# Two-kilobyte rows for the first weight slices, a new order of the start-up and heavier transfer costs in a planned kernel

## The chip, the cores and the metric

The kernel runs on one core of a Trainium2 chip. The core has a matrix engine (TensorE, PE in the profile), a vector engine (DVE), a scalar engine (ACT), GpSimd (POOL) and SyncE (SP), which issues nearly all transfers; 16 DMA engines carry them. The time is device microseconds of one execution; the kernel before took a median of 743.23 us in 3 runs (741.82 to 743.35).

## The reference

Attention between tokens and a small state comes first, in both directions; two dense layers follow. For batch 4, 8 heads, 512 tokens, 32 state rows and head size 64:

```
scores  = scale * x @ state^T          a  = softmax(scores)    xread = a  @ state
scores2 = scale * state @ x^T          a2 = softmax(scores2)   sread = a2 @ x
t   = concat(xread, sread) as [2176, 512]         (4 x 544 rows)
y   = g1(t @ w_in1) @ w_out1          g1(h) = h if h > 0 else exp(h) - 1
out = g2(y @ w_in2) @ w_out2          g2(h) = h * tanh(softplus(h))
```

All four weights are [512, 2048] or [2048, 512] and come as 64-bit floats; activations are 32-bit.

## The kernel before

The tokens' part of the first layer is not computed as written. A head's `a @ state` followed by its rows of `w_in` is `a @ (state @ w_in)`, so the kernel folds the state into the weight (`fold`, L532, result tile `m`) and multiplies the softmax weights (`x1`) by it. The hidden dimension is cut into 16 slices of 128 columns; slice j of `w_in` gives hidden tile h_j (`mm1`), an activation chain on ACT and DVE (`hidden`) turns it into g_j, and `mm2` adds g_j @ w_out slice j into four accumulators.

A slice of `w_in1` is loaded by `weight`: two DMAs, one for partitions 0 to 63 and one for 64 to 127, each of 64 partitions x 4 rows of 128 values (1 KB a row, from a matrix whose rows are 16 KB). Then ACT (`Prelu`, L467), a DVE shift and a DVE merge (L484) make 32-bit floats of the 64-bit words. A `w_out` slice is one DMA over 128 partitions with rows of 4 KB. Raw words go to `raw_in` and `raw_out` tiles; tokens come to `xb` tiles (`load_x`, L565: 128 partitions, rows of 1 KB).

A softmax of one half of the heads of one batch (`token_reads`): transpose tokens on PE (`xT`), scores on PE, then on DVE the maximum, the difference, the sum and the division, `exp` on ACT, a transpose on PE (`pT`) and a copy to `x1`. The raw scores are copied too (`raw`), stored to DRAM (`s2d`) and read again later in the other direction. State rows come through `st_raw` and `st` to the tiles `sd`.

The order of all instructions is written by a planner (`Plan.run`): it simulates the engines with a cost for each operation, picks whichever ready operation can start first (ties by due time), and emits it. A transfer costs its KB times a weight, at 330 KB/us in one line of transfers, plus 2 us; small idle stretches of PE up to plan time 18 are filled with dummy transposes (`gap`). What the planner believes of a transfer therefore sets the order of PE, ACT, DVE and SP, and each engine runs that order strictly. On the chip, eight semaphores take turns with the DMAs, so SP issues a DMA only when the eighth before it has landed.

Of the kernel before, what the change touches and what calls it, by code (L numbers as in the profile page):

```python
# [11 lines left out]
F32 = mybir.dt.float32  # L12
F32R = mybir.dt.float32r
U32 = mybir.dt.uint32
I64 = mybir.dt.int64
AF = mybir.ActivationFunctionType
ALU = mybir.AluOpType
# [5 lines left out]
P = 128  # L23
B, H, S, NS, D = 4, 8, 512, 32, 64
DM, DFF = 512, 2048
ST = S + NS
NK = DM // P
NF = DFF // P
# [29 lines left out]
class Plan:  # L58
# [10 lines left out]
    def add(self, engs, cost, fn, r=(), w=(), due=None, lag=0.0, after=(), place=()):  # L69


        op = Op()
        op.engs = (engs,) if isinstance(engs, str) else engs
        op.cost, op.fn, op.due, op.lag = cost, fn, due, lag
        op.succs, op.end, op.seq = [], None, len(self.ops)
        preds = set(after)
        for k in r:
            if k in self.writer:
                preds.add(self.writer[k])
        for k in w:  # L80
            if k in self.writer:
                preds.add(self.writer[k])
            preds.update(self.readers.get(k, ()))
        for k in w:
            self.writer[k], self.readers[k] = op, []
        for k in r:
            if k not in w:
                self.readers.setdefault(k, []).append(op)
        preds.discard(op)
        op.preds = preds  # L90
        for p in preds:
            p.succs.append(op)
        op.n = len(preds)
        bufs = {}
        for k in (*r, *w):
            k = k[0] if isinstance(k, tuple) else k
            if isinstance(k, Buf):
                bufs[k] = None
        bufs.update((k, None) for k in place)
        op.bufs = list(bufs)  # L100
        for b in op.bufs:
            b.left += 1
        self.ops.append(op)
        return op
# [112 lines left out]
def attention_elu_mish(  # L217
# [18 lines left out]
    nc = tc.nc  # L236
    w_dram = {1: (w_in1, w_out1), 2: (w_in2, w_out2)}
# [3 lines left out]
    def add(*args, after=(), **kw):  # L241
        return plan.add(*args, after=(*after, *gate), **kw)
# [23 lines left out]
    def buf(pool, tag, bufs, shape, dt=F32, name=None):  # L266
        return Buf(pool, tag, bufs, shape, dt, f"{name or tag}{next(serial)}")

    EITHER = ("ACT", "DVE")
# [4 lines left out]
    def copy(e, o, i):  # L274
        (nc.scalar.copy if e == "ACT" else nc.vector.tensor_copy)(o, i)
# [7 lines left out]
    def both(n):  # L283
        return {"ACT": act(n), "DVE": dve(n)}
# [5 lines left out]
    SP, ACTQ = "SP", "ACTQ"  # L290
# [37 lines left out]
    for s, (kind, blk, t0, n, j) in enumerate(steps):  # L328
        c = mm1_cost(kind, blk, n, j) + (mm2_cost(kind, n, whole_out(kind, blk, j)) if kind < 2 else n * 3 * mm(DM))
# [21 lines left out]
    early = True  # L351
# [30 lines left out]
    def A(*args, **kw):  # L382
        op = add(*args, **kw)
        attention.append(op)
        return op
# [46 lines left out]
        return w1[j // 2].t.rearrange("p (k f) -> p k f", k=NK)[:, k, j % 2 * P:(j % 2 + 1) * P]  # L432

    loads = itertools.count()

    def weight(kind, layer, j, due=None):
        i = next(loads)
        soon = i < EARLY
        due = -20.0 + i if i < RAW_FIRST else due
        name = f"{kind}{layer}_{j}_"  # L440
        raw = buf("w", "w_out", NF, [P, DM], I64, "raw_" + name) if soon else \
            buf("work", "wraw", 3, [P, DM], I64, "raw_" + name)
        y = buf("work", "wy", 2, [P, DM], F32, "wy")

        def load():
            if kind == "in":
                cols = w_dram[layer][0][:, j * P:(j + 1) * P]
                if layer == 1:

                    for e in range(2):  # L450
                        nc.sync.dma_start(out=raw[e * D:(e + 1) * D, :].rearrange("p (k f) -> p k f", f=P),
                                          in_=cols.rearrange("(e k d) f -> e d k f", e=2, d=D)[e])
                else:
                    nc.sync.dma_start(out=raw.t.rearrange("p (k f) -> p k f", f=P),
                                      in_=cols.rearrange("(k p) f -> p k f", p=P))
            else:
                nc.sync.dma_start(out=raw.t, in_=w_dram[layer][1][j * P:(j + 1) * P, :])

        def words():
            r = raw.t.bitcast(U32).rearrange("p (f t) -> p f t", t=2)  # L460
            return r[:, :, 1], r[:, :, 0]

        u32 = lambda b: b.t.bitcast(U32)
        add(SP, 512.0, load, w=[raw], due=due)


        add("ACT", 0.68, lambda: nc.scalar.activation(y.t, words()[0].bitcast(F32), AF.Prelu, scale=2.0 ** -112,  # L467
                                                      alpha=2.0 ** 32), r=[raw], w=[y])

        add("DVE", 0.43, lambda: nc.vector.tensor_scalar(u32(y), u32(y), 3, None, ALU.logical_shift_left), r=[y], w=[y])  # L470
        if kind == "in" and layer == 1:
            if j // 2 not in w1:
                w1[j // 2] = buf("w", "w_in", NF, [P, NK * 2 * P], F32, f"w1_{j // 2}_")
            to = w1[j // 2]
            split = lambda t: t.rearrange("p (k f) -> p k f", k=NK)
            out_v, key = lambda: split(to.t.bitcast(U32))[:, :, j % 2 * P:(j % 2 + 1) * P], (to, j % 2)
        elif layer == 1 and j < WHOLE_OUT:
            to = w_sb["whole", layer, j] = buf("w", f"w_{kind}", NF, [P, DM], F32, f"whole{j}_")
            split, out_v, key = (lambda t: t), (lambda: u32(to)), to
            after_step.setdefault(index[1, 0, j], []).append(j)  # L480
        else:
            v = buf("work", "wv", 2, [P, DM], F32, "wv")
            split, out_v, key = (lambda t: t), (lambda: u32(v)), v
        add("DVE", 0.69, lambda: nc.vector.scalar_tensor_tensor(  # L484
            out_v(), split(words()[1]), 29, split(u32(y)), ALU.logical_shift_right, ALU.bitwise_or),
            r=[raw, y], w=[key])
        if kind == "in" and layer == 1 or layer == 1 and j < WHOLE_OUT:
            return
        if layer == 2:
            add(SP, 256.0, lambda: nc.sync.dma_start(out=w2d[:, kind == "out", j, :], in_=v.t),  # L490
                r=[v], w=[("w2d", kind, j)])
            return
        split_weight(kind, layer, j, v)
# [66 lines left out]
    def load_x(b, hf, due=None):  # L560

        t = buf("at", "xb", XB, [P, HH, NC, D], F32, "xb")
        for q in range(2):
            h = hf * HH + 2 * q
            A(SP, 256.0, lambda q=q, h=h: nc.sync.dma_start(  # L565
                out=t[:, 2 * q:2 * q + 2].rearrange("p h c d -> p h (c d)"),
                in_=x[b, h:h + 2].rearrange("h (p c) d -> p h (c d)", c=NC)), w=[(t, q)], due=due, lag=1.0)
        return t
# [11 lines left out]
    def token_reads(b, hf):  # L580
# [7 lines left out]
        if early and hf:  # L588
            xT = buf("w", "w_out", NF, [P, 2, S], F32, "xT")
            prr = buf("w", "w_out", NF, [P, 2, NC, P], F32, "prob")  # L590
            pr, raw = (lambda: prr[:, 0]), (lambda: prr[:, 1])
            kp, kr = (prr, 0), (prr, 1)
            held = [prr]
        else:
            xT = buf("at", "xT", 1, [P, 2, S], F32)
            kp, kr = buf("at", "prob", 1, [P, NC, P], F32), buf("at", "raw", 1, [P, NC, P], F32)
            pr, raw = (lambda: kp.t), (lambda: kr.t)
            held = [kp, kr]
        mx = buf("at", "mx", 2, [P, NC * HH])
# [4 lines left out]
        for q in range(2):  # L604
            pt = bank("xT")
# [9 lines left out]
        if b >= TILES_FROM:  # L615
# [17 lines left out]
            pt = bank("scores")  # L633
# [7 lines left out]
        else:  # L641
            pt = bank("scores")
        for q in range(2 if b < TILES_FROM else 0):
# [8 lines left out]
        all_c = [(pt, q) for q in range(2)]  # L652
        G = NC * HH
        prg = lambda: pr().rearrange("p c (h n) -> p (c h) n", n=NS)
        pv = lambda: pt.t.rearrange("p (g n) -> p g n", n=NS)
        wide = lambda t: t.t.unsqueeze(2).to_broadcast([P, G, NS])
        A("DVE", 0.69, lambda: nc.vector.tensor_reduce(mx.t, pv(), AX.X, ALU.max), r=all_c, w=[mx])
        A("DVE", 0.69, lambda: nc.vector.tensor_tensor(prg(), pv(), wide(mx), ALU.subtract),
          r=all_c + [mx], w=[kp])
        A("ACT", 0.64, lambda: nc.scalar.activation(pr(), pr(), AF.Exp, scale=SCALE), r=[kp], w=[kp], lag=lag)  # L660
        A(EITHER, both(S), lambda e: copy(e, raw().rearrange("p c f -> p (c f)"), pt.t), r=all_c, w=[kr],
          due=T[index[1, b, 0]] + (RAW_DUE if early else -8.0))
        A(SP, 256.0, lambda: nc.sync.dma_start(out=s2d[:, b, hf], in_=raw()), r=[kr], w=[("s2d", b, hf)])
        A("DVE", 0.69, lambda: nc.vector.tensor_reduce(sm.t, prg(), AX.X, ALU.add), r=[kp], w=[sm])
# [298 lines left out]
    early = False  # L963
# [42 lines left out]
    for s in range(len(steps) + 2):  # L1006
        if s < len(steps):
# [4 lines left out]
            h = mm1(s)  # L1012
# [30 lines left out]
TILES_FROM = 4  # L1043
SPLIT_END = True
WHOLE_OUT = 1
X_WEIGHT = 1.5
POOL_LO = set()
RAW_FIRST = 0
FILL, X_DUE = 18.0, -30.0
STATES_DUE, RAW_DUE = 13.0, 5.0  # L1050
EARLY_BANKS = {'warm': 'att', 'st': 'acc2 acc0 acc1', 'xT': 'h h acc0 acc1', 'scores': 'att acc2', 'pT': 'acc0 acc1'}
WARM, EARLY, XB, EBUFS, GBUFS, FOLD_LAG = 14, 8, 3, 2, 2, 5.0

_INS = ["x", "state", "moe_w_in", "moe_w_out", "moe2_w_in", "moe2_w_out"]
# [23 lines left out]
```

## Time and profile before

| | |
|---|---|
| median of 3 runs | 743.23 us |
| the profiled execution | 742.88 us, of which the span of its instructions is 740.7 us |
| PE busy in the span | 730.4 us (99%) |
| DVE, ACT busy | 526.2 us (71%), 427.7 us (58%) |
| granted TensorE clock, mean | 0.997 |

The span runs from the first instruction to the last. A busy PE is a PE with an instruction in it: the dummy transposes and a slow clock count as busy too. The kernel has one dense stream of matmuls after some 22 us of start-up; what the start-up costs shows in the timeline of its first 40 us.

### The profile page before, as it was taken

Reading aid. Unit: us, or ns where it says so; the run is one execution under the profiler, and the core shown is the slowest. Engines: PE = TensorE matmul, PEld = TensorE weight load, DVE = VectorE, ACT = ScalarE, POOL = GpSimd, SP = SyncE. Lnnn points to the kernel's source line nnn. Section 1 sums busy time; section 2 is a strip of 40 time slices with the busy share of each in tenths; the row PEclk is TensorE's granted clock in tenths of the full one; section 3 lists DMA queues with packets and bytes.
Section 4 is the critical chain, followed back from the end, with each engine's and each line's share of the span. In section 5 each row is a group of like instructions: output and inputs, shape, how many; then the busy total and the mean of one; then the engine's idle time right before and its main releaser. Section 6 shows DMA issues by size and latency. Waiting matters only on the chain.

```text
span 740.7 us, 11115 instructions
## 1 busy us (share of the span) xinstructions
PE 730.4 (99%) x4169; PEld 607.0 (82%) x4169; DVE 526.2 (71%) x1001; ACT 427.7 (58%) x767; POOL 9.9 (1%) x25
## 2 busy tenths in 40 slices
PE   7999999999999999999999999999999999999997
PEld 6577877778787879878888888888889999898996
DVE  6888989576788883788897656565566565756555
ACT  4787787555566662676665445554455454545544
POOL 0000000000000000000000000000000000000000
PEclk9999999999999999999999999999999999999999
DMA  9944796152698761874761003000030020001001
GB/s 232 286 135 122 197 282 187 59 156 72 205 281 242 226 208 34 242 217 140 251 203 43 1 1 99 1 1 0 1 100 0 1 73 14 1 1 43 0 1 44
DMA packets 66554, 81.54 MB, mean 110 GB/s; under 512 B 21956, under 2 KB 45252, under 8 KB 66500
## 3 DMA queue, kind: packets, MB, share of 16 engines
q1 hardware_dynamic: 65812, 80.56, 37.1%
q8 instruction: 33, 0.54, 0.3%
q10 hardware_dynamic: 688, 0.26, 0.1%
q14 instruction: 21, 0.17, 0.1%
HBM read 59.31 MB, written 21.50 MB: 109 GB/s over the span
## 4 chain that ended last, share of the span: by engine, by line
PE 97%; DMA 1%; SPq 1%; DVE 0%; ACT 0%; issue 0%
PE acc_acc L873 17%; PE acc_acc L875 16%; PE acc_acc L874 16%; PE h L778 12%; PE h L780 12%; PE h L779 12%; PE fold L532 2%; PE h L754 2%; PE h L764 2%; PE scores L647 1%; DMA st_raw<-in_state 1%; PE gap L364 1%; PE xT L609 1%; PE sr L706 1%; PE acc_att L873 0%; PE acc_att L874 0%
## 5 line engine op out<-in xcount | busy, mean ns | idle before, releaser
L838 ACT CAST g<-e 128x512 fp32r<-128x512 f32 (+2 forms) x148 | 85.8, 580 | 67.1 <-PE acc_acc L875 31.9
L780 PE MATMUL h<-x,w_in 128*128 128x384 f32 (+1 forms) x320 | 114.6, 358 | 0.0
L778 PE MATMUL h<-x,w_in 128*128 128x384 f32 (+1 forms) x320 | 114.4, 358 | 0.0
L779 PE MATMUL h<-x,w_in 128*128 128x384 f32 (+1 forms) x320 | 114.3, 357 | 0.0
L839 DVE TENSOR_TENSOR g<-e,g 128x512 fp32r<-128x512 f32 (+2 forms) x148 | 94.9, 642 | 26.9 <-ACT g L838 26.1
L875 PE MATMUL acc_acc<-w_out,g 128*128 128x512 f32 x272 | 106.8, 393 | 0.0
L874 PE MATMUL acc_acc<-w_out,g 128*128 128x512 f32 x272 | 106.7, 392 | 0.0
L873 PE MATMUL acc_acc<-w_out,g 128*128 128x512 f32 x272 | 105.8, 389 | 0.0
L873 PE MATMUL acc_acc<-g,w_out 128*128 128x512 f32 x252 | 102.0, 405 | 0.0
L875 PE MATMUL acc_acc<-g,w_out 128*128 128x512 f32 x252 | 98.3, 390 | 0.0
L874 PE MATMUL acc_acc<-g,w_out 128*128 128x512 f32 x252 | 98.3, 390 | 0.0
L821 ACT ACTIVATE e<-h 128x384 f32<-128x384 f32 (+2 forms) x81 | 42.9, 530 | 95.4 <-PE h L780 94.2
L830 DVE TENSOR_TENSOR u<-u,e 128x384 f32<-128x384 f32 (+2 forms) x81 | 49.0, 605 | 61.9 <-ACT e L828 61.7
L826 ACT ACTIVATE e<-u,two 128x384 f32<-128x384 f32 (+2 forms) x81 | 53.1, 656 | 53.7 <-DVE u L824 53.6
L778 PEld LDWEIGHTS h<-x,w_in 128*128 128x128 f32 x320 | 60.1, 188 | 7.1
L779 PEld LDWEIGHTS h<-x,w_in 128*128 128x128 f32 x320 | 60.1, 188 | 7.1
L822 DVE TENSOR_SCALAR e<-e 128x384 f32<-128x384 f32 (+2 forms) x81 | 31.0, 383 | 48.5 <-ACT e L821 48.5
L780 PEld LDWEIGHTS h<-x,w_in 128*128 128x128 f32 x320 | 60.0, 188 | 5.0
L875 PEld LDWEIGHTS acc_acc<-w_out,g 128*128 128x128 f32 x272 | 51.0, 188 | 10.8
L806 DVE SCALAR_TENSOR_TENSOR e<-e,h 128x512 f32<-128x512 f32 x67 | 45.7, 683 | 19.3 <-ACT e L799 19.0
L873 PEld LDWEIGHTS acc_acc<-g,w_out 128*128 128x128 f32 x252 | 47.3, 188 | 14.1 <-issue 4.4
L874 PEld LDWEIGHTS acc_acc<-w_out,g 128*128 128x128 f32 x272 | 51.0, 188 | 9.6
(127 smaller groups left out, 1164.6 us busy)
## 6 DMA issues: line engine op xcount, KB each, us to landing
raw_out<-in_moe_w_out SPq DMA_DIRECT2D x32, 512.0 KB, 4.8
raw_in<-in_moe_w_in SPq DMA_DIRECT2D x32, 256.0 KB, 6.0
raw_in<-in_moe_w_in SPq DMA_DIRECT2D x16, 512.0 KB, 4.7
w2d<-wv SPq DMA_DIRECT2D x32, 256.0 KB, 4.1
xb<-in_x SPq DMA_DIRECT2D x16, 256.0 KB, 4.2
x2d<-o SPq DMA_DIRECT2D x16, 256.0 KB, 3.8
xb<-in_x SPq DMA_DIRECT2D x32, 128.0 KB, 4.1
back_in<-w2d SPq DMA_DIRECT2D x16, 256.0 KB, 3.2
```

Source lines behind the costliest of these rows:

```text
L778: nc.tensor.matmul(h[:, :n], lhsT=wh, rhs=xh, start=(k == 0), stop=False)
L779: nc.tensor.matmul(h[:, :n], lhsT=wh, rhs=xl, start=False, stop=False)
L780: nc.tensor.matmul(h[:, :n], lhsT=wl, rhs=xh, start=False, stop=(k == nk - 1))
L806: add("DVE", dve(n), lambda: nc.vector.scalar_tensor_tensor(E(), E(), -1.0, Hh(), ALU.mult, ALU.max), r=[e, h], w=[e])
L821: add("ACT", act(n), lambda c=c: nc.scalar.activation(e[:, c], h[:, c], AF.Exp), r=[h], w=[ke])
L826: add("ACT", act(n) + 0.12, lambda c=c: nc.scalar.activation(e[:, c], u[:, c], AF.Ln, bias=two), r=[ku, "two"], w=[ke])
L830: add("DVE", dve(n), lambda c=c: nc.vector.tensor_tensor(u[:, c], u[:, c], e[:, c], ALU.mult), r=[ku, ke], w=[ku])
L838: add("ACT", act(n) + 0.01, lambda: nc.scalar.copy(g[:, 0, c], e[:, c]), r=r, w=[(g, 0, q)])
L839: add("DVE", dve(n), lambda: nc.vector.tensor_tensor(g[:, 1, c], e[:, c], g[:, 0, c].bitcast(F32), ALU.subtract), r=[*r, (g, 0, q)], w=[(g ...
L873: nc.tensor.matmul(acc.t, lhsT=st[:, 0, :], rhs=mv[:, 0, :], start=fst, stop=False)
L874: nc.tensor.matmul(acc.t, lhsT=st[:, 0, :], rhs=mv[:, 1, :], start=False, stop=False)
L875: nc.tensor.matmul(acc.t, lhsT=st[:, 1, :], rhs=mv[:, 0, :], start=False, stop=lst)
```

## The change

1. The first four slices of `w_in1` are fetched as two pairs: one DMA for each half of the partitions brings 256 columns, so rows are 2 KB and a DMA 512 KB. The pair tiles lie in the two buffers `x` of pool `work`.
2. In `token_reads` the copy of the raw scores may start only after the difference (scores minus maximum) has read them.
3. Planner costs: a `w_in1` slice and the early token loads are weighed 1.45 times their KB, a pair 1.15 times.
4. `EARLY_BANKS`: the third transpose of states (`st`) goes to the PSUM bank of the second (`acc1 acc1`), the second `pT` to `acc2`.

```diff
-        raw = buf("w", "w_out", NF, [P, DM], I64, "raw_" + name) if soon else \
-            buf("work", "wraw", 3, [P, DM], I64, "raw_" + name)
+        pair = kind == "in" and layer == 1 and j < PAIRED
+        if pair:
+            if j % 2 == 0:
+                pairs[j // 2] = buf("work", "x", 2, [P, NK, 2 * P], I64, "raw_" + name)
+            raw = pairs[j // 2]
...
-                cols = w_dram[layer][0][:, j * P:(j + 1) * P]
+                n = 2 * P if pair else P
+                cols = w_dram[layer][0][:, j * P:j * P + n]
...
+                    o = raw.t if pair else raw.t.rearrange("p (k f) -> p k f", f=P)
                     for e in range(2):
-                        nc.sync.dma_start(out=raw[e * D:(e + 1) * D, :].rearrange("p (k f) -> p k f", f=P),
+                        nc.sync.dma_start(out=o[e * D:(e + 1) * D],
                                           in_=cols.rearrange("(e k d) f -> e d k f", e=2, d=D)[e])
...
-        add(SP, 512.0, load, w=[raw], due=due)
+        if not pair:
+            add(SP, 512.0 * (W_WEIGHT if kind == "in" and layer == 1 else 1.0), load, w=[raw], due=due)
+        elif j % 2 == 0:
+            add(SP, 1024.0 * PAIR_WEIGHT, load, w=[raw], due=due)
...
-            A(SP, 256.0, lambda q=q, h=h: nc.sync.dma_start(
+            A(SP, 256.0 * (W_WEIGHT if early else 1.0), lambda q=q, h=h: nc.sync.dma_start(
...
-        A("DVE", 0.69, lambda: nc.vector.tensor_tensor(prg(), pv(), wide(mx), ALU.subtract),
-          r=all_c + [mx], w=[kp])
+        less = A("DVE", 0.69, lambda: nc.vector.tensor_tensor(prg(), pv(), wide(mx), ALU.subtract),
+                 r=all_c + [mx], w=[kp])
...
-        A(EITHER, both(S), lambda e: copy(e, raw().rearrange("p c f -> p (c f)"), pt.t), r=all_c, w=[kr],
+        A(EITHER, both(S), lambda e: copy(e, raw().rearrange("p c f -> p (c f)"), pt.t), r=all_c, w=[kr], after=[less],
...
-X_WEIGHT = 1.5
+X_WEIGHT, W_WEIGHT = 1.5, 1.45
+PAIRED, PAIR_WEIGHT = 4, 1.15
...
-EARLY_BANKS = {'warm': 'att', 'st': 'acc2 acc0 acc1', 'xT': 'h h acc0 acc1', 'scores': 'att acc2', 'pT': 'acc0 acc1'}
+EARLY_BANKS = {'warm': 'att', 'st': 'acc2 acc1 acc1', 'xT': 'h h acc0 acc1', 'scores': 'att acc2', 'pT': 'acc0 acc2'}
```

The changed kernel's lines after the diff's first place lie 8 to 15 numbers higher (L609 becomes L624, L764 becomes L779).

The transfers on SP, from behind the first four token loads (`raw_in_0` is the word tile of slice 0, `st_raw` the states, the later `xb` the tokens of batch 1). Before, beginning with slice 1:

```order
L451 DMA raw_in_1_33_134<-in_moe_w_in 64x4x128 x2
L405 DMA st_raw_143<-in_state 128x6x64
L451 DMA raw_in_2_39_155<-in_moe_w_in 64x4x128 x2
L451 DMA raw_in_3_46_178<-in_moe_w_in 64x4x128 x2
L457 DMA raw_out_0_30_193<-in_moe_w_out 128x512
L457 DMA raw_out_1_35_214<-in_moe_w_out 128x512
L451 DMA raw_in_4_52_240<-in_moe_w_in 64x4x128 x2
L451 DMA raw_in_5_59_254<-in_moe_w_in 64x4x128 x2
L457 DMA raw_out_2_42_264<-in_moe_w_out 128x512
L451 DMA raw_in_6_65_304<-in_moe_w_in 64x4x128 x2
L457 DMA raw_out_3_48_326<-in_moe_w_out 128x512
L565 DMA xb_350<-in_x 128x2x256 x2
```

Now, beginning with the first pair:

```order
L459 DMA raw_in_0_27_131<-in_moe_w_in 64x4x256 x2
L405 DMA st_raw_166<-in_state 128x6x64
L459 DMA raw_in_2_38_168<-in_moe_w_in 64x4x256 x2
L465 DMA raw_out_0_30_204<-in_moe_w_out 128x512
L459 DMA raw_in_4_50_210<-in_moe_w_in 64x4x128 x2
L459 DMA raw_in_5_57_264<-in_moe_w_in 64x4x128 x2
L465 DMA raw_out_1_34_296<-in_moe_w_out 128x512
L465 DMA raw_out_2_41_319<-in_moe_w_out 128x512
L459 DMA raw_in_6_63_341<-in_moe_w_in 64x4x128 x2
L465 DMA raw_out_3_46_368<-in_moe_w_out 128x512
L580 DMA xb_389<-in_x 128x2x256 x2
```

Slices 0 and 1, and 2 and 3, come together; `raw_out_1` moved behind slices 4 and 5. What stands ahead of the tokens of batch 1 is the same set of slices as before.

On ACT, around the conversion of slice 2 (`wy_259` before, `wy_277` now) and the copies of the states (`sd` from `st`). Before:

```order
L660 ACTIVATE prob_196<-prob_196 128x512
L467 ACTIVATE wy_259<-raw_in_2_39_155 128x512
L275 COPY sd_79<-st_225 64x8x32 x2
L275 COPY sd_80<-st_244 64x8x32 x2
L275 COPY sd_81<-st_244 64x8x32
L275 COPY x_0_6_295<-pT_294 128x512
```

Now:

```order
L275 COPY sd_79<-st_270 64x8x32
L482 ACTIVATE wy_277<-raw_in_2_38_168 128x512
L275 COPY sd_79<-st_270 64x8x32
L275 COPY x_0_6_288<-pT_287 128x512
L275 COPY sd_80<-st_302 64x8x32 x2
L482 ACTIVATE wy_321<-raw_in_2_38_168 128x512
```

The second copy out of `st_270` now stands behind the conversion of slice 2; `st_302` is written to the same bank as `st_270`.

On PE, around hidden tile 2 (`h_172` before, `h_170` now). Before:

```order
L764 MATMUL h_172_410<-x_0_6_295,m_0_130_231 128x512 x2
L861 MATMUL acc_0_acc_175_421<-gw_394,whole_32_380 128x512
L861 MATMUL acc_0_acc_176_427<-gw_394,whole_32_380 128x512
L861 MATMUL acc_0_acc_177_436<-gw_394,whole_32_380 128x512
L861 MATMUL acc_0_acc_178_445<-gw_394,whole_32_380 128x512
L764 MATMUL h_180_450<-x_0_6_295,m_0_130_231 128x512 x2
```

Now:

```order
L876 MATMUL acc_0_acc_175_404<-gw_380,whole_32_366 128x512
L876 MATMUL acc_0_acc_176_410<-gw_380,whole_32_366 128x512
L547 MATMUL fold_423<-w_1_40_338,sd_78 32x256
L547 MATMUL fold_424<-w_1_40_338,sd_78 32x256
...
L624 MATMUL xT_443<-ident,xb_389 128x128 x4
L779 MATMUL h_170_450<-x_0_6_288,m_0_128_254 128x512 x2
```

A transpose of the tokens of batch 1 (`xT_443` from `xb_389`) now stands ahead of hidden tile 2. Before, the same four transposes stood behind hidden tile 5.

On PE, around hidden tiles 8 to 10 (`h_207`, `h_211`, `h_219` before; `h_205`, `h_209`, `h_217` now), where block 0's last products (from `g_749`, now `g_757`) are added. Before:

```order
L780 MATMUL h_207_763<-x_1_143_717,ms_625 128x512
L778 MATMUL h_211_802<-x_1_143_717,ms_695 128x512
L779 MATMUL h_211_802<-x_1_143_717,ms_695 128x512
L780 MATMUL h_211_802<-x_1_143_717,ms_695 128x512
L873 MATMUL acc_0_acc_178_445<-g_749,w_out_7_77_776 128x512
L874 MATMUL acc_0_acc_178_445<-g_749,w_out_7_77_776 128x512
L875 MATMUL acc_0_acc_178_445<-g_749,w_out_7_77_776 128x512
L532 MATMUL fold_861<-w_4_80_836,sd_78 32x256
...
L778 MATMUL h_219_882<-x_1_143_717,ms_844 128x512
```

Now:

```order
L795 MATMUL h_205_753<-x_1_141_718,ms_653 128x512
L793 MATMUL h_209_779<-x_1_141_718,ms_701 128x512
L794 MATMUL h_209_779<-x_1_141_718,ms_701 128x512
L795 MATMUL h_209_779<-x_1_141_718,ms_701 128x512
L547 MATMUL fold_825<-w_3_65_463,sd_79 32x256
...
L793 MATMUL h_217_873<-x_1_141_718,ms_846 128x512
```

The last accumulator's three matmuls, which stood between hidden tile 9 and tile 10, now stand ahead of tile 8.

## Rows read from the trace of the kernel before

**Rows 1.** The page: busy time by engine, and the chain that ended last.

```profile
PE 730.4 (99%) x4169; PEld 607.0 (82%) x4169; DVE 526.2 (71%) x1001; ACT 427.7 (58%) x767; POOL 9.9 (1%) x25
...
PE 97%; DMA 1%; SPq 1%; DVE 0%; ACT 0%; issue 0%
```

**Rows 2.** Waits of PE, whole span: who waited for whom, us, times, longest.

```profile
PE st L417 <- ACT st_raw L275: 2.3, 1, 2.3
...
PE h L778 <- DVE e L806: 1.0, 1, 1.0
```

**Rows 3.** Busy time in stretches, with granted clock, DMA share and GB/s.

```profile
core 0: us, PE busy (x) PEld busy (x) DVE busy (x) ACT busy (x) POOL busy (x), PEclk, DMA share, GB/s
6.00:10.00 4.00, 3.57 (x34) 3.33 (x32) 2.53 (x5) 0.68 (x2) 0.12 (x1) 1.00 1.14 224
12.50:15.50 3.00, 1.00 (x20) 0.64 (x21) 1.03 (x2) 2.22 (x5) 0.00 (x0) 1.00 1.14 218
15.90:19.30 3.40, 3.40 (x19) 3.40 (x17) 3.26 (x9) 2.83 (x7) 0.00 (x0) 0.50 1.04 339
31.00:32.40 1.40, 1.40 (x5) 0.61 (x4) 1.40 (x3) 1.40 (x3) 0.00 (x0) 1.00 1.12 388
74.30:77.70 3.40, 3.34 (x15) 2.77 (x16) 3.19 (x9) 2.90 (x6) 0.00 (x0) 1.00 1.05 316
```

**Rows 4.** Issue to landing of single transfers: slice 3's second half, batch 1's first tokens.

```profile
L451 SPq DMA_DIRECT2D raw_in<-in_moe_w_in x1: 1065/1065/1065, 9.6 to 9.6; - x1
...
DMA to landing us min/median/max: 9.1/9.1/9.1
...
L565 SPq DMA_DIRECT2D xb<-in_x x1: 384/384/384, 23.2 to 23.2; - x1
...
DMA to landing us min/median/max: 9.2/9.2/9.2
```

**Rows 5.** Timeline of PE: start, length, instruction, idle before it.

```profile
14.50 0.44 PE L417 MATMUL st<-ident,st_raw 128*128 128x128 f32 x2 [2.33 <-ACT st_raw L275]
...
33.64 1.88 PE L764 MATMUL h<-x,m 128*128 128x512 f32 x4
35.45 0.66 PE L532 MATMUL fold<-w,sd 64*32 64x256 f32 x16
36.04 0.50 PE L873 MATMUL acc_acc<-g,w_out 128*128 128x512 f32 x1
...
38.90 1.88 PE L764 MATMUL h<-x,m 128*128 128x512 f32 x4
...
48.65 1.04 PE L609 MATMUL xT<-ident,xb 128*128 128x128 f32 x8
```

**Rows 6.** The chain that ended last, in order of time: start, us, what.

```profile
15.90 4.39 PE gap L364 x25
20.30 0.44 PE pT L672 x4
20.73 1.09 PE gap L364 x10
...
30.37 3.43 PE acc_acc L861 x8
```

**Rows 7.** Timeline of ACT: conversion of a slice, copies of the states.

```profile
16.95 0.65 ACT L467 ACTIVATE wy<-raw_in 128x512 f32<-128x512 f32 x1
17.50 1.88 ACT L275 COPY sd<-st 64x256 f32<-64x256 f32 x5
```

**Rows 8.** Timeline of PE around the late wait.

```profile
71.94 0.39 PE L873 MATMUL acc_acc<-g,w_out 128*128 128x512 f32 x1
...
72.39 0.39 PE L875 MATMUL acc_acc<-g,w_out 128*128 128x512 f32 x1
72.71 0.66 PE L532 MATMUL fold<-w,sd 64*32 64x256 f32 x16
74.36 0.50 PE L778 MATMUL h<-x,ms 128*128 128x512 f32 x1 [0.99 <-DVE e L806]
```

More of the change, by code (lines that the diff above doesn't have):

```diff
@@ L434, in attention_elu_mish @@
     loads = itertools.count()
+    pairs = {}
     def weight(kind, layer, j, due=None):
@@ L440, in weight @@
         name = f"{kind}{layer}_{j}_"
-        raw = buf("w", "w_out", NF, [P, DM], I64, "raw_" + name) if soon else \
-            buf("work", "wraw", 3, [P, DM], I64, "raw_" + name)
+        pair = kind == "in" and layer == 1 and j < PAIRED
[3 more added lines that the diff above has]
+            raw = pairs[j // 2]
+        else:
+            raw = buf("w", "w_out", NF, [P, DM], I64, "raw_" + name) if soon else \
+                buf("work", "wraw", 3, [P, DM], I64, "raw_" + name)
         y = buf("work", "wy", 2, [P, DM], F32, "wy")
@@ L459, in words @@
         def words():
+            if pair:
+                r = raw.t.bitcast(U32).rearrange("p k (f t) -> p k f t", t=2)[:, :, j % 2 * P:(j % 2 + 1) * P]
+                return r[:, :, :, 1], r[:, :, :, 0]
             r = raw.t.bitcast(U32).rearrange("p (f t) -> p f t", t=2)
@@ L463, in weight @@
         u32 = lambda b: b.t.bitcast(U32)
-        add(SP, 512.0, load, w=[raw], due=due)
-        add("ACT", 0.68, lambda: nc.scalar.activation(y.t, words()[0].bitcast(F32), AF.Prelu, scale=2.0 ** -112,
+        cut = lambda t: t.rearrange("p (k f) -> p k f", k=NK) if pair else t
+        if not pair:
+            add(SP, 512.0 * (W_WEIGHT if kind == "in" and layer == 1 else 1.0), load, w=[raw], due=due)
+        elif j % 2 == 0:
+            add(SP, 1024.0 * PAIR_WEIGHT, load, w=[raw], due=due)
+        add("ACT", 0.68, lambda: nc.scalar.activation(cut(y.t), words()[0].bitcast(F32), AF.Prelu, scale=2.0 ** -112,
                                                       alpha=2.0 ** 32), r=[raw], w=[y])
@@ L484, in weight @@
         add("DVE", 0.69, lambda: nc.vector.scalar_tensor_tensor(
-            out_v(), split(words()[1]), 29, split(u32(y)), ALU.logical_shift_right, ALU.bitwise_or),
+            out_v(), words()[1] if pair else split(words()[1]), 29, split(u32(y)), ALU.logical_shift_right, ALU.bitwise_or),
             r=[raw, y], w=[key])
```

## The prediction

> **What bounds the kernel now.** I read the page first: PE is busy for 730.4 of 740.7 us, and 97% of the chain that ended last is PE [rows 1]. Then the waits of PE: only two matter to this change, 2.3 us at `st` for ACT and 1.0 us at a hidden tile for DVE [rows 2]. So nothing here is gained by making a transfer, ACT or DVE faster as such. The time moves only where PE waits, where it fills time with dummy transposes, or where its clock is low, and all of that lies in the first 35 us and at 74 us. The stretches [rows 3] show the rest: the DMA engines are taken throughout the start, a stretch in which PE ran at half clock (15.9 to 19.3 us, granted 0.50), and full clock after the late wait. The chain [rows 6] shows the dummies: 25 in 4.39 us, then 10 in 1.09 us, before the first hidden tile at 21.8 us. Last come the timelines of PE [rows 5, 8] and ACT [rows 7] around the places where the order changes, and issue and landing of two transfers that PE will meet [rows 4].
>
> The sum is made against the profiled execution, 742.88 us, of which 740.7 is span; the median of the runs is 743.23, 0.35 higher. I take the difference from the first and give the forecast against the second.
>
> **1. Pairs instead of slices.** The bytes ahead of batch 1's tokens on SP are the same, so the question is the price of a byte. Stretches in which only slices of 64 partitions move (1 KB rows) give 224 and 218 GB/s. The stretch with batch 1's tokens, which also have 1 KB rows but go to 128 partitions, gives 388 [rows 3]. So a row of 1 KB does not keep a transfer at 220; of what the rows differ in, the 64 partitions remain, and a pair has them too. Two bounds follow for a pair of 1.049 MB: 4.7 us at 224 GB/s (no gain) and 2.7 us at 388 (2.0 us gained on each pair). I take no gain, because the 388 row excludes the row length as the limit and nothing else in the DMA changes. Then the second pair lands whole when slice 3's second half does now, 9.6 + 9.1 = 18.7 us [rows 4], and batch 1's first tokens again at 23.2 + 9.2 = 32.4 us. Slice 0, which landed alone, now comes with slice 1, one slice's transfer later (0.524 MB at 224 GB/s, 2.3 us); that is not on the path, since its fold stands behind dummies.
>
> [...]
>
> **2. The start, up to the first hidden tile.** The third `st` now shares a bank with the second, and the second copy out of that bank (`sd_79`) stands on ACT behind the conversion of slice 2. That conversion waits for the whole pair (18.7 us), takes 0.65, and one copy 1.88/5 = 0.38 [rows 7]. So the third `st` starts at about 19.7. Dummies end earlier, and PE waits there about 2 us. Behind it stand four state transposes, four `pT` transposes (0.44 each group by [rows 6]), and the first hidden tile starts at about 20.6, instead of 21.8. This puts PE 1.2 us ahead; the earlier wait of 2.33 us at `st` [rows 5] is filled by 29 dummies.
>
> **3. The transpose of batch 1 ahead of hidden tile 2.** This is the step that decides. Before, from the first hidden tile to the one at 33.64 PE needs 33.6 − 21.8 = 11.8 us [rows 5, 6]. Out of this comes what after does not have ahead of the transpose: one hidden tile, 35.45 − 33.64 = 1.81, and one `pT`, 0.44. That leaves 9.6, so PE reaches the transpose at about 20.6 + 9.6 = 30.2, up to 0.9 later if ACT's copies hold it. The tokens land at 32.4. PE waits 1.3 to 2.2 us, with all of the stream behind it: this eats the 1.2 us of step 2 and more. From 32.4: transpose 0.44; tile 2, 1.81; fold, 36.04 − 35.45 = 0.59; tile 3, 1.81; twelve products, 38.90 − 36.04 = 2.86 [rows 5]. Tile 4 starts at 39.9 or 40.0, against 38.90 before: +1.05. The four transposes that before stand behind tile 5 (at 48.65, of eight [rows 5]) are then done: −0.44. Net **+0.6**. The bounds: if the tokens came as soon as PE is there, −2.2 from this, so −1.6; a second token DMA that is late by a slot would add about 1.
>
> **4. The late wait.** Before tile 10 PE waits 0.99 us for DVE's `e` [rows 8]: tile 10 takes a PSUM buffer that is free when tile 8's chain (exponential and relu on ACT, the merge `e` on DVE) has read it. Between tiles 9 and 10 stood the last three products, which begin 0.22 to 0.23 apart (71.94 and 72.39 for the first and the third): 0.68 of work that lay in that chain's shadow. Now they stand ahead of tile 8, so tile 8 and its chain come 0.68 later, while PE is at tile 10 when it was before. The wait grows by as much: **+0.7**, to 1.7. The lower end is 0: if ACT starts tile 8's exponential late for work of its own, the later tile costs nothing. I take the upper, since row and order both have DVE's merge as the last to end and its chain hangs on the tile.
>
> **5. Raw copies behind the difference.** A copy of 0.69 us by the planner's cost moves on DVE or ACT behind the difference. PE is still making scores for other heads there and is 3.57 of 4.00 us busy between 6 and 10 us [rows 3]; the store `s2d` is read long after. Cost 0. Without that cover it would be one copy, +0.7.
>
> Sum: 742.88 + 0.6 + 0.7 = 744.2 for a profiled execution, 744.5 against the median.
>
> **Rivals.** *A, the pairs are faster.* If 2 KB rows raise the rate from 224 towards 388, the tokens land up to 4 us earlier and step 3's wait goes; PE is then held by the fold and the copies at about 30.0 to 30.5 at the transpose instead of 32.4. Tile 4 starts about 2 us earlier than in the forecast, −1.3 in step 3; with +0.7 at 74 us the sum is −0.6, and with none there −1.3: 742.6 and 741.9 against the median, 742.3 taken. For it: rows are the only thing that changes in a packet. Against it: 388 GB/s at 1 KB rows.
>
> *B, the clock falls: slower.* PE fell to half clock after 2.33 us of idleness at 12.2 to 14.5 (0.50 from 15.9 to 19.3) and stayed at full clock after 0.99 us (1.00 from 74.3) [rows 3, 5, 8]. The new idle stretches are near 2 us at the third `st`, 1.3 to 2.2 before the transpose, and 1.7 at tile 10. They lie between the two cases, so either may hold. The price: 25 dummies took 4.39 us at half clock, at full clock they take 25 × 1.09/10 = 2.7 [rows 6], so 1.7. If the fall comes in front of real matmuls, as after the transpose, the sum is 744.5 + 1.7 = 746.2. If it comes only at the third `st`, it is absorbed by the wait for the tokens. The clock rose at 19.3 behind a stretch of dummy transposes. [...]
>
> *C, no late wait.* Step 4 at its lower end: 743.8. It stays on the forecast's side.
>
> **How the numbers follow.** About 0.2%, 1.5 us, is what a measurement of this kernel can tell from no change; the bounds are 741.74 and 744.72. The forecast, with C in it, has 0.44 and reaches from 743.5 to 745.3; about 0.27 of that lies within 0.2%, 0.17 above. A has 0.28: 0.12 below 741.74, by its far end where more slices gain and none of it is lost at 74 us, 0.16 within. B has 0.28, nearly all above. So faster 0.12, same 0.44, slower 0.44. The likeliest is the forecast, 744.5. The range of eight in ten leaves the far half of A and the far end of B out: 742.0 to 746.4.
>
> **What would show it.** Right: PE idle 1.3 to 2.2 us before `xT` at 30 to 32 us for the DMA of `xb`; tile 4 near 40 us; some 1.7 us of waiting at tile 10; the pairs at about 220 GB/s. Step 1 is wrong if the second pair lands well before 18.7; step 4 if tile 10 waits no more than 1 us; step 2 if the third `st` starts well off 19.7. A granted clock of 0.5 in a stretch behind `xT` is B. The forecast falls if the tokens of batch 1 land before 31 us.

## The result and the profile after

The changed kernel took a median of 748.28 us in 7 runs (744.86 to 749.61), the kernel before 742.61 in 7 runs (741.82 to 743.68): a ratio of 1.0065, interval 1.0049 to 1.0080. It is slower, by 4.8 us by that ratio and by 5.7 us between the medians. The forecast was 744.5, the range 742.0 to 746.4: the side was right, the size was not. The profiled execution of after has a span of 747.2 us, 6.5 more than before's 740.7.

The page and the waits of PE after (total, times, longest), beside [rows 1, 2]:

```profile
PE 733.0 (98%) x4172; PEld 607.0 (81%) x4172; DVE 529.5 (71%) x1011; ACT 422.4 (57%) x757; POOL 9.0 (1%) x25
```

```profile
PE xT L624 <- DMA xb<-in_x: 3.4, 1, 3.4
PE fold L547 <- ACT m L275: 2.0, 1, 2.0
PE st L417 <- ACT sd L275: 1.5, 1, 1.5
...
PE h L793 <- DVE e L821: 1.4, 1, 1.4
```

The 3.4, the 1.5 and the 1.4 were forecast, as 1.3 to 2.2, about 2, and 1.7. The 2.0 at a fold was not. The timeline of PE (start, length, instruction, idle before it) shows where they lie:

```profile
29.05 0.62 PE L547 MATMUL fold<-w,sd 64*32 64x256 f32 x2
31.71 0.66 PE L547 MATMUL fold<-w,sd 64*32 64x256 f32 x14 [2.04 <-ACT m L275]
35.78 1.09 PE L624 MATMUL xT<-ident,xb 128*128 128x128 f32 x4 [3.41 <-DMA xb<-in_x]
36.66 3.62 PE L779 MATMUL h<-x,m 128*128 128x512 f32 x4
40.21 0.83 PE L547 MATMUL fold<-w,sd 64*32 64x256 f32 x16
...
45.57 1.88 PE L779 MATMUL h<-x,m 128*128 128x512 f32 x4
```

Tile 2 takes 3.62 us where one took 1.88 in [rows 5]. The stretches after (PE, PEld, DVE, ACT and POOL busy, granted clock, DMA share, GB/s) say why:

```profile
12.50:15.50 3.00, 3.00 (x40) 2.57 (x39) 2.96 (x7) 2.38 (x7) 0.00 (x0) 1.00 1.08 216
15.90:19.30 3.40, 1.85 (x18) 1.62 (x16) 2.42 (x6) 1.86 (x4) 0.00 (x0) 1.00 1.06 271
31.00:32.40 1.40, 0.66 (x14) 0.18 (x14) 1.05 (x3) 0.68 (x3) 0.00 (x0) 1.00 1.12 265
32.40:35.60 3.20, 0.00 (x0) 0.00 (x0) 3.16 (x7) 1.41 (x3) 0.00 (x0) 0.72 1.07 246
35.80:40.90 5.10, 5.10 (x24) 2.10 (x24) 0.14 (x1) 1.73 (x3) 0.00 (x0) 0.53 0.85 299
```

At 15.9 to 19.3 the clock is now 1.00 (0.50 in [rows 3]); it falls in the idle stretch before the transpose, at 33.8, and is at half until 40.6 (0.53 granted from 35.8 to 40.9). Pairs run at 216 GB/s, where single slices ran at 218.

The fold waits for ACT's copy of `m`. ACT's timeline shows the copy (at 31.07) behind a conversion of `raw_out` that waits for its DMA:

```profile
27.75 0.57 ACT L275 COPY m<-fold 128x512 f32<-128x512 f32 x1
30.00 0.66 ACT L482 ACTIVATE wy<-raw_out 128x512 f32<-128x512 f32 x1 [1.68 <-DMA raw_out<-in_moe_w_out]
30.56 0.61 ACT L853 CAST g<-e 128x512 fp32r<-128x512 f32 x1
31.07 0.59 ACT L275 COPY m<-fold 128x512 f32<-128x512 f32 x1
```

And the tokens: issued at 23.2 as before, landed 12.5 us later, not 9.2 [rows 4]:

```profile
L580 SPq DMA_DIRECT2D xb<-in_x x1: 385/385/385, 23.2 to 23.2; - x1
...
DMA to landing us min/median/max: 12.5/12.5/12.5
```

### The profile page after: what moved, and what is told of

Read it like the earlier page. It is cut to its first block, busy times and chain, and to the rows that moved or that the text cites. A ratio compares the mean times of both kernels' runs of the same rounds, so it can differ in the third digit from the quotient of the medians.

```text
span 747.2 us, 11119 instructions
## 1 busy us (share of the span) xinstructions
PE 733.0 (98%) x4172; PEld 607.0 (81%) x4172; DVE 529.5 (71%) x1011; ACT 422.4 (57%) x757; POOL 9.0 (1%) x25
## 4 chain that ended last, share of the span: by engine, by line
PE 94%; DMA 4%; SPq 0%; ACT 0%; DVE 0%; issue 0%
PE acc_acc L888 16%; PE acc_acc L890 16%; PE acc_acc L889 16%; PE h L793 12%; PE h L795 12%; PE h L794 12%; DMA xb<-in_x 2%; PE fold L547 2%; DMA raw_in<-in_moe_w_in 2%; PE h L769 2%; PE scores L662 1%; PE h L779 1%; PE xT L624 1%; PE sr L721 1%; PE acc_att L889 0%; PE acc_att L890 0%
## 5 line engine op out<-in xcount | busy, mean ns | idle before, releaser
L890 PEld LDWEIGHTS acc_acc<-w_out,g 128*128 128x128 f32 x272 | 51.0, 188 | 10.8
L821 DVE SCALAR_TENSOR_TENSOR e<-e,h 128x512 f32<-128x512 f32 x67 | 45.9, 684 | 19.5 <-ACT e L814 19.1
L889 PEld LDWEIGHTS acc_acc<-w_out,g 128*128 128x128 f32 x272 | 51.0, 188 | 9.6
L888 PEld LDWEIGHTS acc_acc<-w_out,g 128*128 128x128 f32 x272 | 51.1, 188 | 9.2
```

What stands on the lines that cost most here:

```text
L821: add("DVE", dve(n), lambda: nc.vector.scalar_tensor_tensor(E(), E(), -1.0, Hh(), ALU.mult, ALU.max), r=[e, h], w=[e])
L888: nc.tensor.matmul(acc.t, lhsT=st[:, 0, :], rhs=mv[:, 0, :], start=fst, stop=False)
L889: nc.tensor.matmul(acc.t, lhsT=st[:, 0, :], rhs=mv[:, 1, :], start=False, stop=False)
L890: nc.tensor.matmul(acc.t, lhsT=st[:, 1, :], rhs=mv[:, 0, :], start=False, stop=lst)
```

## What the experiments asked

At first there were two theories. Theory 1: PE waits for batch 1's tokens because their transpose now stands ahead of tile 2, and the clock falls behind the wait. Theory 2: the pairs' transfers delay one DMA engine. A third came out of the first four runs. In before's order on PE slices 2 and 3 are folded for batch 0 (`w_1` with `sd_78`, for tiles 2 and 3) and then slices 0 to 3 for batch 1 (`sd_79`), which are needed late. In after it is the other way round: batch 1's folds stand behind tiles 0 and 1, and the fold for tiles 2 and 3 comes last, at 29.05.

```profile
22.19 0.66 PE L547 MATMUL fold<-w,sd 64*32 64x256 f32 x16
...
24.70 0.66 PE L547 MATMUL fold<-w,sd 64*32 64x256 f32 x16
```

The folds have two PSUM buffers; batch 1's folds fill both, the copies that free them are late on ACT, and the fold that tile 2 needs waits for the second buffer. The transposes of later tokens take their PSUM buffers from the same two. Theory 3: this inversion is the cause, and the early transpose a part of what follows from it.

"Ratio" is to the kernel before, run beside each. `hold` in the edits is the earliest plan time at which the planner may start an operation; the planner then orders everything else anew.

**The changed kernel again** (again; no edit).

> The changed kernel once more, for a second profile and for its spread. Theory 1 (the order): PE waits for the tokens of batch 1 at the transpose that now stands ahead of hidden tile 2, and where that idle stretch is long the clock falls to half behind it. So its runs fall into two groups by the mean clock: near 745.4 us where it is 0.998, near 748.8 where it is 0.995 or less; the median 745 to 749. Theory 2 (the pairs): transfers of 2 KB rows leave one DMA engine 3 to 4 us behind the others in every run; the lag of the tokens' landing is the same in the new profile, 35 to 36 us, and the runs do not fall into two groups.

747.91 us, ratio 1.0075 (1.0053 to 1.0097). The runs spread from 744.4 to 751.1; those at a mean clock of 0.996 or 0.997 took 744.4 and 747.7, that at 0.993 took 751.1: no two groups, but the longest has the lowest clock. The tokens landed at 35.6 again, so the late landing is not an accident of one run. Both are what theory 2 expected here.

**Transposes held back** (held).

```diff
-            A("PE", NC * (0.11), turn, ...)
+            setattr(A("PE", NC * (0.11), turn, ...), "hold", HOLD if b == 1 and not hf else 0.0)   # HOLD = 45
```

> The changed kernel, with the four transposes of batch 1's first tokens held back in the plan until behind hidden tile 5, as before; pairs, banks and weights stay. Theory 1: no wait for these tokens and no half clock behind it, so 5 us come back and the earlier first tile shows: 743.0 us (741.5 to 744.3), no granted clock of 0.5 between 30 and 42 us. Theory 2: the late engine delays the slices and w_out too, and PE waits for those: 746 to 749.

746.92 us, ratio 1.0060 (1.0046 to 1.0075): 1.4 us less than the changed kernel by the medians, and the intervals overlap. Theory 1 falls as the whole cause. The time lies in theory 2's range, and late transfers have a part in it: ACT's copy of `m` stands here too behind a conversion of `raw_out` that waits 1.2 us for its DMA. PE itself waits for no transfer. It waits twice at folds for ACT's copies of `m`, in the same place, and the clock still falls (mean 0.82 from 21 to 40 us):

```profile
29.86 0.62 PE L547 MATMUL fold<-w,sd 64*32 64x256 f32 x2
31.86 0.66 PE L547 MATMUL fold<-w,sd 64*32 64x256 f32 x14 [1.39 <-ACT m L275]
34.07 1.11 PE L547 MATMUL fold<-w,sd 64*32 64x256 f32 x16 [1.55 <-ACT m L275]
```

**Pairs fetched in rows of 1 KB** (split_pair). Order and plan as in the changed kernel, four DMAs a pair.

```diff
-                    for e in range(2):
+                    for f, e in [(f, e) for f in range(n // P) for e in range(2)]:
```

> The changed kernel in its own order, but each pair is fetched by four DMAs of 1 KB rows (as slices were before) instead of two of 2 KB rows. Theory 1: the order is at fault and the wait stays: 745 to 749 us, PE waiting 1.3 to 3.5 us at the transpose. Theory 2: the pairs' DMAs are at fault: the lag goes back to what it was before (tokens landed at 32.4 us), 743 to 744.7.

748.50 us, ratio 1.0077 (1.0065 to 1.0090), tokens landed at 34.9. Theory 2 falls as far as it rests on the rows: their length is not at fault, and 2 KB rows show no gain (212 GB/s here from 12.5 to 15.5 us, 216 in after).

**Dummies before the transpose** (filled).

```diff
             def turn(q=q, pt=pt):
+                fill(pt, FILLS if b == 1 and not hf and not q else 0)   # FILLS = 24
```

> The changed kernel with 24 more dummy transposes (2.6 us at full clock) right ahead of the transpose that waits for batch 1's tokens: the wait stays, but PE is not idle in most of it. Theory 1 with half clock as the greater part of the loss: the clock stays at 1.00 behind the transpose and about 2.4 us come back: 745.5 (744.5 to 746.5), all runs at a clock of 0.997 or more. If the lost time is the wait alone and the clock costs nothing: 748 to 750.

750.31 us, ratio 1.0100 (1.0080 to 1.0120). It doesn't tell what it was made for: the dummies need the transposes' PSUM buffer, which ACT's copy of `m` frees only at 33.6, so they began behind the idle time and ran mostly at half clock themselves (0.58 granted from 34 to 38 us). It tells something else: tokens landed at 32.4 would have had to wait for that buffer as well.

```profile
33.60 4.51 PE L364 MATMUL xT<-ident 128*128 128x128 f32 x24 [1.50 <-ACT m L275]
37.95 0.60 PE L625 MATMUL xT<-ident,xb 128*128 128x128 f32 x4
38.38 1.88 PE L780 MATMUL h<-x,m 128*128 128x512 f32 x4
```

Behind them tile 2 runs at full clock (1.88), but the next fold begins at 40.20, as in the changed kernel (40.21): the dummies paid for the clock what the tile would have paid.

**Batch 1's folds held back** (fold_first).

```diff
-            A("PE", 0.1 + mm(4 * step * P), ...)
+            o = A("PE", 0.1 + mm(4 * step * P), ...); o.hold = HOLD if b else 0.0   # HOLD = 24
```

> The changed kernel, with the folds for batch 1 held back in the plan until 24 us, so that slices 2 and 3 are folded for batch 0 (hidden tiles 2 and 3) first, as in the kernel before. Theory 3 (the folds): in the changed kernel batch 1's folds come first and hold both PSUM buffers of the folds; their copies stand on ACT behind conversions that wait for late w_out words, so PE waits 2 us at the fold for tiles 2 and 3 and reaches the transpose late and idle. Then this kernel has PE dense from the first tile on: 741.0 to 743.3 us, no wait over 0.5 us between 21 and 40 us and no half clock there. Theory 1 (the transpose alone): no gain over the kernel with the transposes held back, 746 to 748.

741.73 us, ratio 0.9994 (0.9983 to 1.0005). The order takes back the whole loss, with pairs, weights, banks and the rule on raw copies all in place. The edit holds the folds of batches 1 to 3; in the new plan batch 1's stand at tile 7, and the transposes are back behind tile 5 too. Held has the transposes there as well, so what lies between the two (746.9 and 741.7) is the folds and what the plan moves with them. The tokens still land at 35.6, `raw_out_2` still at 30.1; nobody waits for them. PE is not quite as dense as was expected: it waits 0.8 us for DVE's `gw` at 27.3, and the clock did fall, at the start, behind the 2.0 us at `st` (0.53 from 19.6 to 22.3):

```profile
PE st L417 <- ACT sd L275: 2.0, 1, 2.0
PE warm L360 <- DVE ident_cols L336: 1.5, 1, 1.5
PE acc_acc L876 <- DVE gw L818: 0.8, 1, 0.8
```

**Parts of the change undone.** In this order: the banks of before (banks); the raw copies without their rule (noless); all slices single, `PAIRED = 0` (unpaired). The edit shown is that of banks.

```diff
-EARLY_BANKS = {..., 'st': 'acc2 acc1 acc1', ..., 'pT': 'acc0 acc2'}
+EARLY_BANKS = {..., 'st': 'acc2 acc0 acc1', ..., 'pT': 'acc0 acc1'}
```

> The changed kernel with the PSUM banks of the kernel before (acc2 acc0 acc1 and acc0 acc1). In its order the fold of slices 2 and 3 for batch 0 stands ahead of batch 1's folds and the transpose of batch 1 stands behind tile 5. Theory 3 (the folds): the loss goes, 742.0 to 744.0 us. Theory 1 in its weak form, that late landings alone cost the time, whatever the folds do: 745.5 to 748.

> The changed kernel without the rule that the raw copies stand behind the difference. In its order the transpose of batch 1 is back behind tile 5, but batch 1's folds still stand ahead of the fold of slices 2 and 3 for batch 0. Theory 3 (the folds): the wait at that fold stays, 745.5 to 748 us. Theory 1 (the transpose): 742 to 744.

> The changed kernel with all slices fetched singly (no pairs), weights, banks and the raw copies' rule as in it. In its order the transpose stands behind tile 5, and batch 1's folds ahead of the fold of slices 2 and 3 for batch 0. Theory 3 (the folds): 745.5 to 748 us. Theory 1 (the transpose) and theory 2 (the pairs): 742 to 744.

745.97 (1.0053, 1.0031 to 1.0075), 747.20 (1.0064, 1.0048 to 1.0080) and 744.81 us (1.0030, 1.0014 to 1.0045). The last two still have the folds inverted, and most of their waiting is at the folds (2.7 and 3.8 us for ACT's `m`, each in two waits), though the transposes stand behind tile 5; unpaired came out 0.7 below what was expected. The profile of noless is of an execution of 743.92 us, 3.3 under its median, at a mean clock of 1.000 (the others: 0.994 to 0.997). Banks is a miss for theory 3: with the folds in before's order it was still slow, in the range of theory 1's weak form. But PE waits for no transfer in it. Its waits are 2.5 us at `pT` for ACT's `sd`, with a fall of the clock behind it (0.76 granted from 15.9 to 22 us), 0.8 and 0.7 at the first tiles, and 1.4 at tile 10. So the inversion goes when the banks are undone and stays without the rule or the pairs, and the folds in order are not enough: taking a part back gives the plan other bad places. The weights were not undone by themselves.

**The inversion, in the kernel before** (before_late_fold). Only the fold of slices 2 and 3 for batch 0 is held until 22.5 us in the plan.

```diff
+            o.hold = HOLD if (b, j0) == (0, 2) else 0.0   # HOLD = 22.5
```

> The kernel before, with one thing changed: the fold of slices 2 and 3 for batch 0 may not start ahead of 22.5 us in the plan. Batch 1's folds then come first, and the plan itself puts the transpose of batch 1 ahead of tile 2, as in the changed kernel; transfers up to batch 1's tokens stand in their order of before, without pairs, new weights or new banks. Theory 3 (the folds): the whole loss appears without any part of the change: 745.5 to 750 us, with PE waiting for ACT's copy of m and for the tokens between 28 and 38 us. If the pairs, weights or banks have a cost of their own (late landings), this kernel stays near its source: 742 to 744.5.

748.18 us, ratio 1.0084 (1.0058 to 1.0111): the loss of the change, without any part of it. But the edit moves more than the folds: the plan by itself then puts the transposes ahead of tile 2. They wait for the PSUM buffer that ACT's copy of `m` frees, and the tokens land at the same moment, 32.3. The profile puts the wait down to the copy; this run does not tell the two apart.

```profile
PE xT L609 <- ACT m L275: 2.4, 1, 2.4
PE st L417 <- ACT st_raw L275: 2.0, 1, 2.0
...
PE h L778 <- DVE e L806: 1.0, 1, 1.0
PE fold L532 <- DVE m L275: 0.9, 1, 0.9
PE acc_acc L874 <- DVE g L839: 0.7, 1, 0.7
```

```profile
31.21 1.06 ACT L275 COPY m<-fold 128x512 f32<-128x512 f32 x2
```

```profile
32.40 0.63 PE L609 MATMUL xT<-ident,xb 128*128 128x128 f32 x4 [2.37 <-ACT m L275]
```

The profile is of an execution of 746.7 us, 1.5 under the median, at a mean clock of 0.998 (the others: 0.993 to 0.996).

**What the parts are worth with the folds in order.** fold_first with one part undone or changed, in this order: without the rule on raw copies (fold_noless), without pairs (fold_unpaired), a pair weighed 1.25 (fold_pw125) and 1.35 (fold_pw135).

> Batch 1's folds held back until 24 us as in fold_first, and the raw copies without their rule (as before). Theory 3 (the folds): again no wait at the folds and none for the tokens, 741 to 743.5 us; against the 747.2 of the same kernel without the hold this is 4 us or more. If the rule on the raw copies was worth something by itself, it is over 742.5; if it cost, below 741.5.

> Batch 1's folds held back until 24 us, and all slices fetched singly. Theory 3 (the folds): 741 to 743.5 us. Beside fold_first (741.7) it shows what the pairs are worth by themselves: if 2 KB rows gain nothing, the two are within 1 us; if they gain, this one is over 742.7.

> fold_first with a pair weighed 1.25 times its KB in the plan instead of 1.15: the copies of the states come ahead of slice 2's conversion on ACT or go to DVE, and the last products of slice 0 are moved behind tile 4 or 5. Theory 3: as fold_first or better, since its wait of 2.0 us at the third state transpose is shorter: 740.0 to 742.5 us. If that start is hidden behind later landings all the same: 741.5 to 743.5.

> fold_first with a pair weighed 1.35 times its KB. In its order the transposes of batch 1 stand ahead of tile 5. Theory 3: 740.0 to 742.5 us if the tokens (landing near 36 us) are there when PE comes to them at about 37 us; if PE waits for them, 743 to 746, with a wait at the transpose.

741.06 (0.9978, 0.9967 to 0.9989), 740.01 (0.9965, 0.9951 to 0.9979), 743.37 (1.0012, 0.9998 to 1.0025) and 743.63 us (1.0015, 0.9999 to 1.0031). The first two beat both kernels. fold_unpaired is the best: 2.8 us under before, no wait at `st` and full clock from 21 to 40 us:

```profile
PE warm L360 <- DVE ident_cols L336: 1.5, 1, 1.5
PE acc_acc L876 <- DVE gw L818: 1.0, 1, 1.0
PE h L793 <- DVE e L821: 0.8, 1, 0.8
```

So the pairs, with what the plan makes of them, cost 1.7 us here (741.73 to 740.01; the intervals of the ratios do not meet), which neither branch of the expectation had. Most of it can be the start: fold_first waits 2.0 us at `st` and then runs at half clock, fold_unpaired does neither. Neither heavier weight gained; both lie in the slower branch of their expectation. The first got waits of 1.5 us for ACT's `x` and 1.2 for `sd`, the second 2.6 us in two waits at the transposes for the tokens, which is theory 1 in small.

The two gains together (fold_unpaired_noless):

> Batch 1's folds held back until 24 us, slices fetched singly, raw copies without their rule: the two fastest versions so far in one. If their gains come from different waits: 738.5 to 740 us. If they come from the same idle time at the start: 740 to 741.5.

748.18 us, ratio 1.0056 (1.0037 to 1.0075), far outside both branches. The two gains do not add: in this plan one of batch 1's folds comes ahead of tile 2 again, and a transpose waits 2.9 us for ACT's `m`, then runs slow (1.11 for what takes 0.60):

```profile
41.41 1.11 PE L624 MATMUL xT<-ident,xb 128*128 128x128 f32 x4 [2.94 <-ACT m L275]
43.20 1.12 PE L624 MATMUL xT<-ident,xb 128*128 128x128 f32 x4 [0.68 <-ACT xT L275]
```

## Why the prediction was wrong

Step 1 held in its rate: pairs run at 216 GB/s, and rival A is dead. The second pair was whole at 17.6, 1.1 us before the forecast's 18.7, but not by a faster transfer: before, the last of the sixteen parts of slice 3 came 1.5 us behind the fifteenth (17.2 and 18.7), now 0.1 us. Step 2 held: the third `st` began at 18.87 (forecast 19.7), the first tile at 19.80 (20.6). Step 5, a cost of 0, is not settled: without the rule, with the folds in order, the time was 741.06 instead of 741.73, which by the expectation for fold_noless is a cost of the rule, but the intervals of the two ratios overlap.

Step 3 is the step that failed, in two terms of its sum and in the rival that was to catch a third. Tile 4 began at 45.57, against 39.9 or 40.0.

- "The tokens land at 32.4": they landed at 35.65. The transpose began at 35.78, 3.4 later. Not all of this is the tokens': by filled, the buffer for the transpose was not free before 33.6, so 1.2 us of it would have been lost to ACT's copy in any case.
- The half clock of rival B came, and in the place that the rival named: from 35.78 to 40.98, 5.2 us for work of 0.44 + 1.81 + 0.59 = 2.84 at full clock. It cost 2.4; the rival had 1.7.
- 1.05 forecast + 3.4 + 2.4 = 6.8; measured 45.57 − 38.90 = 6.7. With −0.44 for the transposes and +0.4 at tile 10 (1.4 against 0.99, step 4 forecast 0.7) this is 6.6 of the 6.5 in the span.
- "Up to 0.9 later if ACT's copies hold it": ACT held the fold for 2.04. In the sum this is hidden under the late tokens. But it is the root: the prediction added 0.59 for each fold, looked at which folds there were and not at which came first, and did not ask which buffers they wait for. Without the tokens' wait most of the loss stayed (held: 746.9); with the folds in order it went (741.7). The inversion put into the kernel before made a loss as large (748.2), there together with the early transposes. The late landings have their share, since ACT's copies stand behind conversions that wait for them, but with the folds in order the same lateness costs nothing that shows (fold_first). How the loss divides between the two was not measured.

So the forecast named the right place and a true wait, but took a consequence for the cause. The chance of B (0.28) was too low, since its condition, a longer idle stretch, was bound up with the landing that the forecast took as known from one profile. Even B's 746.2 was too low, for the same landing.

Open is why the tokens land 3.3 us late. Bytes explain little: from 17.6 to 32.4 us the DMA engines moved 273 GB/s instead of 285, 0.18 MB less, 0.8 us at 224 GB/s. A transfer has landed when the last of its sixteen parts has, and the profile marks each: before, the eighth part of this transfer is done at 30.8, the fifteenth at 32.0 and the last at 32.4; after, at 31.1, 32.2 and 35.7. One part lags, from the first `raw_out` on, and it makes `raw_out_2` late as well (the fifteenth part at 27.1, the last at 29.9), for which ACT waits ahead of the copy of `m`. For these tokens it is 2.0 to 3.6 us behind the fifteenth in eleven of the fourteen profiles of the changed kernel and its variants, 0.9 to 1.1 in the other three (noless, unpaired, fold_unpaired_noless), and 0.4 and 1.0 in before and before_late_fold. Splitting the pairs left it, and fold_unpaired has it without any pair. One lead stands in the traces. A fetch of the program's instructions (the profile's queue q8), one packet of 16 KB, begins at 17.67 in after and takes 1.11 us, and the first transfer to lag is the one that lands next (its fifteenth part at 19.1, its last at 21.0). In the eleven profiles this fetch begins at 16.9 to 17.9, in the three others at 16.4, 19.8 and 20.6, in before and before_late_fold at 19.0 and 18.2. That is no more than a coincidence in time: the lag is longer than the fetch and grows after it (in after 1.9 us at that transfer, 3.5 at the tokens), and no run moved the fetch.

## What to carry to other kernels

When a planner's costs change, read the new order for two things before adding up durations: what is needed late but now comes before what is needed soon, and which small pool of buffers both use. A copy that frees such a buffer is on the path as soon as it stands, on an in-order engine, behind an instruction that waits for a transfer (here ACT's conversion waited 1.68 us for `raw_out`, and PE 2.04 at the fold for the copy behind it). A forecast wait that ends with a landing time read from one profile should carry a spread of some microseconds (the tokens came 3.3 later here). An idle stretch of about 2 us or more, behind which the clock may fall (here it fell in or behind ones of 1.99, 2.33 and 3.41 us, and not behind ones of 2.30 and 2.37), should be priced in the forecast, not beside it.

## What the runs showed of the hardware

The clock fell to half behind an idle stretch of 1.99 us (fold_first) and stayed at full behind one of 1.55 (after, at the same instruction; granted from 19.6 to 22.3 us 0.53 and 1.00); before, it fell behind 2.33 and stayed behind 0.99 [rows 3, 5, 8]. That is no limit between 1.55 and 1.99, though: it stayed at full behind 2.30 in held, at the same instruction (below: the four transposes behind it took 0.60), behind 2.37 in before_late_fold (1.00 from 32.4 to 40 us) and behind 2.2 in fold_pw135 (mean clock of the profiled execution 0.999). The length of one idle stretch does not decide, so rival B's condition could not be read off it.

```profile
19.69 0.66 PE L417 MATMUL st<-ident,st_raw 128*128 128x128 f32 x4 [2.30 <-ACT sd L275]
20.18 0.60 PE L687 MATMUL pT<-ident,prob 128*128 128x128 f32 x4
```

It rose again while PE did nothing but dummy transposes: in filled 24 of them took 4.51 us from 33.6 us on, with 0.58 granted from 34 to 38 us, and the transposes behind them took 0.60 for four, where the same four took 1.09 at half clock in after. And in after, where dummies fill the 2.33 us in which PE idled before, the clock is at 1.00 from 15.9 to 19.3 (0.50 in [rows 3]). Transfers to 64 partitions at a time show no gain from longer rows: 224 and 218 before and 219 and 203 in unpaired with rows of 1 KB, 228 and 216 in after with rows of 2 KB (GB/s from 6 to 10 and from 12.5 to 15.5 us), and from 12.5 to 15.5 us 212 in split_pair, with rows of 1 KB again.
